# A 2-D transform and token update on one core: third stage on the four corners of the array, whole token rows stored, shorter loads, early scores for the last pair

## The chip, the core and the metric

The kernel runs on one of the cores of a Trainium2 chip. A core has five engines with queues of their own, executed in order: TensorE (PE, matrix multiplies into PSUM; its weight loads are shown as PEld), VectorE (DVE), ScalarE (ACT), GpSimd (POOL) and SyncE (SP, which here only issues DMAs). Sixteen DMA engines move data between HBM and SBUF. The metric is the device time of one execution in microseconds (us), the median of the runs.

## What is computed

```python
def _attn_ref(x):                      # x: (8, 3136, 256) float32
    X = np.fft.fft(x, axis=1)
    X = np.fft.fft(X, axis=2)
    return X.real.astype(np.float32)

def _moe_ref(x, w_gate, w1, w2, capacity):   # x is the transform, capacity 128
    scores = np.einsum('bsd,d->bs', x, w_gate)
    out = x.copy()
    for b in range(B):
        top_idx = np.argpartition(-scores[b], capacity)[:capacity]
        xe = x[b, top_idx]
        ye = np.maximum(xe @ w1, 0.0) @ w2
        g = 1.0 / (1.0 + np.exp(-scores[b, top_idx]))
        out[b, top_idx] = x[b, top_idx] + g[:, None] * ye
    return out
```

## The kernel before

The token axis of 3136 is split into 64 x 49, which needs no twiddle factors, so a batch passes three stages of matmuls, all in fp32. The input is laid out on the host: partitions are 98 rows (49 positions, twice) and 30 rows of zeros, and four tiles `x` of 1 MB make one batch.

- **Loads and folds.** `loads` brings the tiles over SP's queue into six buffers. `folds` adds the two mirrored halves of a tile (L319; DVE for batch 0, POOL for the others), in place.
- **Stage 1** (L346): per batch 66 pairs of matmuls, 128 rows x 64 columns, with `w1d` of 100 columns; the two of a pair write the upper and lower half of the PSUM partitions. ACT copies eight chunks to `uv` (L347, L349).
- **Stage 2** (L373): 25 values of k, two matmuls each (again the two halves of the columns) with `cuv` of 130 columns, three k in one PSUM bank. The copy to `s2` (L378) goes to DVE and ACT in turn.
- **Stage 3** (L389): one 128 x 128 matmul with 390 columns for each three k, with the table `mm`, which holds the 64 x 64 table `a` four times, `[[a, a], [-a, a]]`. ACT (L391) and DVE (L393) bring the two halves of the columns to the output buffer `o`; L393 adds the offsets `dl` that two small matmuls of stage 1 made.
- **Leave** (L412): twelve DMAs per batch write `o` to HBM, 64 partitions each and pieces of 512 bytes, half a token row. After them come the scores `sc` of the batch (L417), which one column of `o` holds, and their way to HBM and back (`spill`, `scr`, L419, L453), which spreads them for the search.
- **Search** (streams A to D, one for each pair of batches): six rounds of counting the scores over a threshold (ACT for A to C, L486; DVE for D, L489), a small matmul (L496) and a comparison; then the chosen rows' numbers are put in order (`chosen`, L584).
- **FFN** (streams a to d): the chosen rows are gathered from the output in HBM (L595), go through 96 matmuls of 256 columns and are scattered back (L642).

The order of all this is one string, `ORDER`: each letter lets one stream issue its next piece (l load, f fold, s, p, q stages 1 to 3, o leave, w weights, A to D, a to d). Every engine's queue follows from it. Stage 2 and stage 3 have two PSUM banks each.

Of the kernel before, what the change touches and what calls it, by code (L numbers as in the profile page):

```python
# [24 lines left out]
R = 132  # L25
LOW = 64 * K2
BIG = 3.0e38
RAD = {1: (16, 6), 2: (16, 6), 4: (8, 8)}
XBUFS, UVBUFS, OBUFS = 6, 2, 2
GROUPS = [[0, 1], [2, 3], [4, 5], [6, 7]]  # L30
PAIRS = [[0, 1], [2, 3], [4, 5], [6, 7]]
WARMS = 0
CORNERS = 4
TRIPLES = [(k, min(k + 3, K2)) for k in range(0, K2, 3)]
STORES = [(0, 9), (9, 18), (18, 25)]
ORDER = "3flflfl2slf2sl2slwfsl2fsfsl2psfq2s2p2fpfq2sp2qlpq2fqflso2sloqfsp2sqpfpfsqsqopsosl2f2pqpsofqs2posoqfposfsqlwl2qoqspf2psfofpqfpwsosql2qofpqp2olA2sfqsfqpAplqlspspqs2flAsoAslAlfqpfoAqwps2AospAfAf2qs2pAloslAwfqfqAoAfsos3Aopsqspf2qAf2pfpsAwqp2sqApAosfwpsoqwqpfsp2owqflaqowasqwof2spaqpqopsl2pfwsfqBlaqplflfqwaqpfpopBaqBqoqaplaBspsfalasofsBoaBaBsofsBlasBo2sq2oBapsBafBofpBsqfqpofqBsos2BafqoBpfs2aoBspaBqopCqBapBapCb2qoCsbf2qbopsbfsobqso2posbqCpCopCqCqoCpb2CpqaCqCbpoCqopCqobo2CbpC2qobCobobC3bCDbCbDbDbDcbc2Dc2Dc2D2c2Dc2Dc2Dc2DcbD2c2Ddcd6cdcd2c18d"
# [5 lines left out]

CHUNKS = [(1 + 4 * i, min(5 + 4 * i, 32)) for i in range(8)]
# [26 lines left out]
def _rows():  # L70

    p, c = np.arange(128)[:, None], np.arange(K2)[None]
    place = np.where(p >= 64, LOW + (p - 64) * (K2 - 1) + c - 1, p * K2 + c)
    k = np.arange(S)
    k1, k2 = k % NT, k % NB2
    mir = k2 >= K2
    return place, np.where(mir, LOW + -k1 % NT * (K2 - 1) + NB2 - k2 - 1, k1 * K2 + k2)


def _tables():  # L80
# [5 lines left out]
    t["w1d"] = np.concatenate([np.concatenate([c, -s, s, c], 1), np.concatenate([c, -s, -s, -c], 1), np.zeros((30, 100))], 0)  # L86
    d = np.arange(128)[:, None]
    k3 = np.array([0] + EO)[None]
# [4 lines left out]
    cu[:, 0] = 0  # L93
# [63 lines left out]
def kernel(ctx: ExitStack, tc: tile.TileContext, x, w1, w2, wgr, tb, outs, groups, pairs):  # L157
# [5 lines left out]
    xp = ctx.enter_context(tc.tile_pool(name="xp", bufs=XBUFS))  # L163
# [6 lines left out]
    ps3 = ctx.enter_context(tc.tile_pool(name="ps3", bufs=2, space=bass.MemoryType.PSUM))  # L170
# [4 lines left out]
    def bank(name, pool):  # L175
        return pool.tile([128, 512], F32, tag="bank", name=name)
# [8 lines left out]

    def loads():
        for b in range(NB):
            for i in range(4):
                t = xp.tile([128, 2, 8 * 128], F32, tag="x", name=f"x_{b}_{i}")
                src = x[4 * b + i].rearrange("p (c w) -> p c w", c=2)  # L190
                for c0, c1 in ((0, 1), (1, 2)) if b == 0 else ((0, 2),):
                    nc.sync.dma_start(t[:, c0:c1], src[:, c0:c1])  # L192
                    tiles[b, i] = t
                    yield True


    wz = cp.tile([128, 512], F32, tag="wz", name="wz")
    nc.vector.memset(wz, 0.0)
    wb = cp.tile([128, 128], BF16, tag="wb", name="wb")
    nc.vector.memset(wb, 0.0)  # L200

    pz = [bank(f"pz{i}", ps1) for i in range(2)]
    for i in range(CORNERS):
        for r in range(2):
            for c in range(2):
                h, w = (slice(64 * r, 64 * r + 64), slice(64 * c, 64 * c + 64))
                nc.tensor.matmul(pz[r][w, 0:260], wz[h, 0:64], wz[h, 64:324], start=True, stop=True)

    w1d = const("w1d", [128, 100], tb["w1d"], nc.scalar)
# [3 lines left out]
    load = loads()  # L213
    next(load)
    next(load)
    next(load)
    cuv = const("cuv", [128, 260], tb["cuv"])
    next(load)
    wgb = const("wgb", [128, 256 + 258], wgr.broadcast_to([128, 256 + 258]))
    next(load)  # L220
    zcs = const("zcs", [33, 256], tb["zcs"])
    mm = const("mm", [128, 128], tb["m"])
# [11 lines left out]

    obuf = [cp.tile([128, K2, R], F32, tag=f"o{i}", name=f"o{i}") for i in range(OBUFS)]
    dlt = [cp.tile([128, K2], F32, tag=f"dl{i}", name=f"dl{i}") for i in range(OBUFS)]
# [4 lines left out]
    wodd = cp.tile([128, 1], F32, tag="wodd", name="wodd")  # L241
    late, hots, se = {}, [], {}
# [15 lines left out]
    def late_setup():
        late["sm"] = const("sm", [128, SMW], tb["sm"])
# [459 lines left out]
```

## Time and profile before

| | us |
|---|---|
| median of 3 runs (284.11 to 285.78) | 284.39 |
| profiled execution | 284.24 |
| its span, first to last instruction | 282.5 |
| PE busy (with PEld beside it) | 239.5 (187.2) |
| DVE, ACT, POOL busy | 129.1, 120.1, 103.4 |

Busy time of PE is the union of its instructions, which are pipelined: a busy PE need not be at its peak. The profiled execution is 1.7 us longer than its span and stands 0.15 us below the median, so the span's times can be used for the median as they are. PE's granted clock is 2.4 GHz where the profile shows 1.0 (9 in tenths, also for a full slice) and 1.2 GHz where it shows 0.5.

### The profile page before, as it was taken

How to read it: one execution, taken by the hardware profiler on the slowest of the kernel's cores; microseconds unless marked ns; L12 is line 12 of the kernel's file. 1: busy time of each engine (PE TensorE's matmuls, PEld its weight loads, DVE VectorE, ACT ScalarE, POOL GpSimd, SP SyncE). 2: the span in 40 equal slices, each digit the busy share in tenths (PEclk: the TensorE clock that was granted, in tenths of full speed). 3: DMA queues.
4: the chain of work that ended last, by engine and by line, in shares of the span. 5: the costliest groups of instructions: out<-in, count | busy, mean ns of one | idle time of the engine just before them, and what ended most of it. 6: DMA issues, size and time to landing. Idle time of an engine off the chain costs nothing.

```text
span 282.5 us, 6641 instructions
## 1 busy us (share of the span) xinstructions
PE 239.5 (85%) x2604; PEld 187.2 (66%) x2604; DVE 129.1 (46%) x429; ACT 120.1 (43%) x292; POOL 103.4 (37%) x132
## 2 busy tenths in 40 slices
PE   4299999999986988999999899999897835568993
PEld 2297668767655665875779777767566724458893
DVE  0531222334325445756753265673557448762340
ACT  2064455545545674557546765234773001100220
POOL 0057953416037770590447471361000611002202
PEclk9579999999996899999999999999999975755998
DMA  6999899789999999999999999987888830000101
GB/s 230 408 421 392 331 240 283 227 236 321 264 298 391 379 367 352 298 225 232 285 346 347 303 277 263 246 224 179 210 194 214 209 97 20 0 0 19 41 19 37
DMA packets 61931, 66.55 MB, mean 236 GB/s; under 512 B 3947, under 2 KB 55884, under 8 KB 58316
## 3 DMA queue, kind: packets, MB, share of 16 engines
q1 hardware_dynamic: 60988, 63.99, 73.5%
q0 software_dynamic: 768, 2.10, 2.4%
q8 instruction: 20, 0.33, 0.5%
q10 hardware_dynamic: 144, 0.05, 0.1%
q14 instruction: 11, 0.09, 0.1%
HBM read 39.28 MB, written 26.84 MB: 234 GB/s over the span
## 4 chain that ended last, share of the span: by engine, by line
PE 32%; issue 23%; DMA 23%; POOL 8%; DVE 6%; ACT 4%; SPq 2%; POOLq 1%; DVEq 0%; ACTq 0%
DMA x<-in_x 15%; PE p L389 8%; PE p L373 8%; PE p L346 6%; DMA out<-o 5%; POOL x L319 4%; PE ph L230 2%; POOL hot L556 2%; PE ph L232 2%; PE ph L231 2%; DVE junk L489 2%; POOL out L642 1%; DMA spill<-sc 1%; ACT junk L486 1%; SPq L192 1%
## 5 line engine op out<-in xcount | busy, mean ns | idle before, releaser
L319 POOL TENSOR_TENSOR x<-x 128x512 f32<-128x512 f32 (+1 forms) x56 | 68.6, 1244 | 58.4 <-DMA x<-in_x 57.5
L346 PE MATMUL p<-w1d,x 128*64 128x100 f32 x1056 | 58.2, 262 | 8.8 <-DVE x L319 7.6
L346 PEld LDWEIGHTS p<-w1d,x 128*64 128x64 f32 x1056 | 50.9, 144 | 19.7 <-issue 14.5
L389 PE MATMUL p<-s,mm 128*128 128x390 f32 x144 | 59.1, 509 | 0.5 <-DVE o L393 0.5
L373 PE MATMUL p<-cuv,uv 128*64 128x130 f32 x800 | 57.3, 282 | 1.4 <-ACT uv L349 0.7
L373 PEld LDWEIGHTS p<-cuv,uv 128*64 128x64 f32 x800 | 44.0, 138 | 15.8 <-issue 8.7
L347 ACT COPY uv<-p 128x400 f32<-128x400 f32 x64 | 36.7, 578 | 39.8 <-PE p L346 36.1
L393 DVE TENSOR_TENSOR o<-p,dl 128x192 f32<-128x192 f32 (+1 forms) x72 | 24.2, 343 | 52.9 <-ACT o L391 51.3
L391 ACT COPY o<-p 128x198 f32<-128x198 f32 (+1 forms) x72 | 23.1, 329 | 30.3 <-PE p L389 26.2
L389 PEld LDWEIGHTS p<-s,mm 128*128 128x128 f32 x144 | 23.0, 192 | 15.1 <-issue 5.2
L378 DVE COPY s<-p 128x390 f32<-128x390 f32 x32 | 18.0, 563 | 25.5 <-PE p L373 25.1
L230 PE MATMUL ph<-xh,w1h 128*128 128x256 f32 x64 | 22.9, 358 | 4.4 <-DVE hl L630 3.5
L378 ACT COPY s<-p 128x390 f32<-128x390 f32 (+1 forms) x40 | 17.7, 441 | 16.2 <-PE p L373 15.6
L556 POOL TENSOR_TENSOR hot<-oa,sm 128x400 bf16<-128x400 bf16 x6 | 7.6, 1288 | 42.2 <-DVE oa L548 42.2
L230 PE MATMUL py<-w2h,hh 128*128 128x256 f32 x64 | 20.5, 321 | 2.0 <-DVE hl L630 1.4
L629 ACT ACTIVATE hh<-ph 128x512 fp32r<-128x512 f32 x16 | 9.5, 595 | 25.8 <-PE ph L232 23.2
L230 PEld LDWEIGHTS ph<-xh,w1h 128*128 128x128 f32 x64 | 13.7, 215 | 9.6 <-DVE hl L630 5.0
L232 PE MATMUL ph<-xl,w1h 128*128 128x256 f32 x64 | 20.0, 312 | 0.0
L595 POOL DMA_INDIRECT xe<-out,chosen x8 | 8.4, 1052 | 31.4 <-DVE chosen L584 28.9
L231 PE MATMUL ph<-xh,w1l 128*128 128x256 f32 x64 | 19.9, 311 | 0.0
L486 ACT ACTIVATE junk<-scr,thr 128x800 bf16<-128x800 f32 x18 | 17.3, 960 | 5.6 <-DVE thr L501 3.3
L630 DVE SCALAR_TENSOR_TENSOR hl<-ph,hh 128x512 fp32r<-128x512 f32 x16 | 11.1, 691 | 17.9 <-ACT hh L629 17.8
(117 smaller groups left out, 288.5 us busy)
## 6 DMA issues: line engine op xcount, KB each, us to landing
x<-in_x SPq DMA_DIRECT2D x28, 1024.0 KB, 10.6
out<-o SPq DMA_DIRECT2D x48, 288.0 KB, 7.0
out<-o SPq DMA_DIRECT2D x32, 224.0 KB, 5.1
x<-in_x SPq DMA_DIRECT2D x8, 512.0 KB
out<-o SPq DMA_DIRECT2D x16, 256.0 KB, 6.2
scr<-spill SPq DMA_DIRECT2D x8, 200.0 KB, 3.5
w1s<-in_w SPq DMA_DIRECT2D x1, 1024.0 KB
w2s<-in_w SPq DMA_DIRECT2D x1, 1024.0 KB
```

The source lines that it names most:

```text
L230: nc.tensor.matmul(out, ah, bh, start=start, stop=False)
L231: nc.tensor.matmul(out, al, bh, start=False, stop=False)
L232: nc.tensor.matmul(out, ah, bl, start=False, stop=stop)
L319: eng.tensor_tensor(t[:, 0 : n * 128], t[:, 0 : n * 128], t[:, n * 128 : 2 * n * 128], op=ALU.add)
L346: nc.tensor.matmul(ps[c : c + 64, q], t[:, s * 128 + c : s * 128 + c + 64], w1d, start=True, stop=True)
L347: nc.scalar.copy(uvt[:, :, :, :, a0:a1], src[:, :, :, :, 0:n])
L373: nc.tensor.matmul(ps[64 * h : 64 * h + 64, 130 * (k - k0) : 130 * (k - k0) + 130], uv[:, h, k], cuv[:, 0:130] if h else cuv[:, 130:260], ...
L378: (nc.vector.tensor_copy if k0 % 2 else nc.scalar.copy)(s2[:, 0 : 130 * n], ps[:, 0 : 130 * n])
L389: nc.tensor.matmul(ps, mm, mids.pop((b, k0))[:, 0 : 130 * n], start=True, stop=True)
L391: nc.scalar.copy(o[:, k0:k1, 0:R:2], pv[:, :, 0:66])
L393: nc.vector.tensor_tensor(o[:, k0:k1, 3:130:2], pv[:, :, 66:130], dl[:, k0:k1].unsqueeze(2).to_broadcast([128, n, 64]), op=ALU.add)
L486: nc.scalar.activation(junk, scr, AF.Sign, bias=thr, scale=-1.0, accum_out=ct)
```

## The change

- **Stage 3 on corners.** A 64 x 64 matmul uses one corner of the array: the upper or the lower rows, the left or the right columns. The table is now `a` alone, twice. For six k (two banks of stage 2) four corner matmuls of 390 columns make two products in two PSUM banks, `pp` and `pq`; ACT copies `pq` to `vt`, and DVE forms `pp - vt` and `pp + vt` into `o`, two instructions of 390 columns each. The two banks are all that stage 3 has: they have one buffer each, where the kernel before turned over two.
- **Offsets earlier.** The offsets are added as stage 2 leaves PSUM (ACT copies 65 columns of each k, DVE adds the offsets to the other 65). For batches 6 and 7 ACT does both.
- **Whole rows.** Rows of `o` and of the output have 260 elements. A batch leaves in six DMAs: two that write 1664 rows in runs of 7,280 or 6,240 bytes for each of 128 partitions, and four that write the 1536 mirrored rows in pieces of 520 bytes.
- **Loads without zero rows.** From batch 2 on, a tile's 98 rows are loaded alone (four DMAs of 64, 32, 1 and 1 rows, to every second, every fourth, and two single partitions); the six buffers keep the zeros of the first two batches.
- **Early scores.** For batches 6 and 7 the scores come from `uv` directly: 50 matmuls of one column, four corner matmuls, two DVE instructions, behind stage 1. Their `spill` goes out before the batch's stores.
- **Search D** counts half of the scores on ACT and half on DVE.
- **Beside these:** the residues of the weights are formed on POOL instead of DVE; 66 dummy bf16 matmuls stand at the start where 16 fp32 corner matmuls on zeros stood (L207); the score columns are made after the first folds; `ORDER` is another string.

```diff
 def loads():
+                if b < WHOLE: ...                                  # as before
+                else:
+                    f = t.rearrange("p c w -> p (c w)")
+                    r = 128 * 4 * WHOLE + 98 * (4 * (b - WHOLE) + i)
+                    nc.sync.dma_start(f[0:128:2], x[r : r + 64])
+                    nc.sync.dma_start(f[1:128:4], x[r + 64 : r + 96])
+                    for q in range(2):
+                        p = ROWS[96 + q]
+                        nc.sync.dma_start(f[p : p + 1]..., x[r + 96 + q : r + 97 + q]...)
 def stage1():
+            if b in EARLY:
+                ps = bank(f"pe_{b}", ps1)[:, 0:K2]
+                for k in range(K2):
+                    for h in range(2):
+                        c = 129 if h else 259
+                        nc.tensor.matmul(ps[64 * h : 64 * h + 64, k : k + 1], uv[:, h, k], cuv[:, c : c + 1], start=True, stop=True)
+                nc.vector.scalar_tensor_tensor(se_, zzb[b % 2], wodd, ps, op0=ALU.mult, op1=ALU.add)
+                yield True
...
+                scored(b)
 def stage3():
-                nc.tensor.matmul(ps, mm, mids.pop((b, k0))[:, 0 : 130 * n], start=True, stop=True)
-                nc.scalar.copy(o[:, k0:k1, 0:R:2], pv[:, :, 0:66])
-                nc.vector.tensor_tensor(o[:, k0:k1, 3:130:2], pv[:, :, 66:130], dl..., op=ALU.add)
+                pp, pq = (bank(f"p3{t}_{b}_{j0}", ps3, t)[:, 0 : R * n] for t in "pq")
+                for c in range(w // 64):
+                    s2 = mids.pop((b, j0 + c * (KH - 1)))
+                    for r, t in enumerate((pp, pq)):
+                        h = slice(64 * r, 64 * r + 64)
+                        nc.tensor.matmul(t[64 * c : 64 * c + 64], mm[h, 0:64], s2[h, 0 : R * n], start=True, stop=True)
+                nc.scalar.copy(vt, pq[0:w])
+                for h, op in enumerate((ALU.subtract, ALU.add)):
+                    nc.vector.tensor_tensor(o[0:w, j0:j1, h]..., pv, vv, op=op)
 def leave():
-                        nc.sync.dma_start(rows[s][h, :, k0 - s : z - s], o[p : p + 64, k0:z, 3 - h : 131 - h])
+                nc.sync.dma_start(rows[:, a:z], o[:, a:z].rearrange("p k h c -> p k (h c)"))
+                for h in range(2):
+                    nc.sync.dma_start(mirrored[h, :, m - 1 : z - 1], o[:, m:z, 1 - h])
```

In PE's queue, where batch 1 is in stages 2 and 3 and batch 2 in stage 1 (`p1_`, `p2_` and `p3_` are the PSUM tiles of the stages, the first number behind them the batch), the kernel before has one wide matmul of stage 3 at a time:

```order
L346 MATMUL p1_2_1_541<-w1d_114,x_2_0_285 64x100 x8
L389 MATMUL p3_1_0_551<-s2_1_0_522,mm_132 128x390
L373 MATMUL p2_1_3_557<-cuv_123,uv_1_313 64x130 x6
L346 MATMUL p1_2_2_566<-w1d_114,x_2_1_407 64x100 x8
L346 MATMUL p1_2_3_578<-w1d_114,x_2_1_407 64x100 x8
L373 MATMUL p2_1_6_593<-cuv_123,uv_1_313 64x130 x6
L373 MATMUL p2_1_9_602<-cuv_123,uv_1_313 64x130 x6
L389 MATMUL p3_1_3_611<-s2_1_3_564,mm_132 128x390
```

Now four corner matmuls stand together, behind two pieces of stage 2 of which they take the results, and serve six k:

```order
L428 MATMUL p2_1_1_683<-cuv_126,uv_1_352 64x130 x6
L428 MATMUL p2_1_13_693<-cuv_126,uv_1_352 64x130 x6
L377 MATMUL p1_2_4_703<-w1d_116,x4_93 64x100 x8
L428 MATMUL p2_1_4_715<-cuv_126,uv_1_352 64x130 x6
L460 MATMUL p3p_1_1_730<-s2_1_1_690,mm_130 64x390
L460 MATMUL p3q_1_1_731<-s2_1_1_690,mm_130 64x390
L460 MATMUL p3p_1_1_730<-s2_1_13_700,mm_130 64x390
L460 MATMUL p3q_1_1_731<-s2_1_13_700,mm_130 64x390
L428 MATMUL p2_1_16_740<-cuv_126,uv_1_352 64x130 x6
```

In SP's queue at the end, before (`out_6`, `out_7`: the output of batches 6 and 7; `spill` and `scr`: the scores' way; `scr_3`: those of search D):

```order
L412 DMA out_6<-o0_134 64x9x128 x2
L412 DMA out_6<-o0_134 64x8x128 x2
L412 DMA out_6<-o0_134 64x9x128 x4
L412 DMA out_6<-o0_134 64x7x128 x4
L419 DMA spill_146<-sc3_141 128x25
L412 DMA out_7<-o1_135 64x9x128 x2
L412 DMA out_7<-o1_135 64x8x128 x2
L412 DMA out_7<-o1_135 64x9x128 x4
L412 DMA out_7<-o1_135 64x7x128 x4
L419 DMA spill_146<-sc3_141 128x25
L453 DMA scr_3_2737<-spill_146 64x1x800 x2
```

and now, from the last tile's load on:

```order
L205 DMA x1_90<-in_x 64x2048
L206 DMA x1_90<-in_x 32x2048
L209 DMA x1_90<-in_x 1x2048 x2
L477 DMA out_6<-o0_134 128x1820
L481 DMA out_6<-o0_134 128x6x130
L358 DMA spill_146<-sc3_141 128x25
L526 DMA scr_3_2950<-spill_146 64x1x800 x2
L481 DMA out_6<-o0_134 128x6x130
L477 DMA out_6<-o0_134 128x1560
L481 DMA out_6<-o0_134 128x6x130 x2
L477 DMA out_7<-o1_135 128x1820
```

The scores of search D leave ahead of all stores of batch 7 and of most of batch 6, where they stood behind them; the last load stands directly before the first store of batch 6, where before all loads were out two batches of stores earlier.

## Rows read from the trace of the kernel before

**Rows 1.** The head of the page: the span, the busy times of the engines, and PE's granted clock in tenths in 40 slices of 7.06 us.

```profile
span 282.5 us, 6641 instructions
...
PE 239.5 (85%) x2604; PEld 187.2 (66%) x2604; DVE 129.1 (46%) x429; ACT 120.1 (43%) x292; POOL 103.4 (37%) x132
...
PEclk9579999999996899999999999999999975755998
```

**Rows 2.** Table by stretches: the stretch, its length, busy us of PE, PEld, DVE, ACT and POOL (with instruction counts), and last the granted clock, the mean busy share of the DMA engines and what they moved in GB/s. In the first two stretches only loads move, in the third loads and stores, in the last two stores (and the short transfers of a search).

```profile
7.00:16.00 9.00, 3.52 (x42) 3.54 (x44) 5.52 (x15) 1.14 (x2) 1.72 (x3) 0.55 1.04 411
18.50:27.00 8.50, 7.84 (x136) 6.63 (x132) 0.93 (x2) 4.61 (x12) 7.78 (x8) 1.00 1.03 396
60.20:69.50 9.30, 9.23 (x114) 7.03 (x114) 3.64 (x11) 4.66 (x12) 3.79 (x4) 1.00 1.00 321
192.00:207.40 15.40, 13.08 (x127) 9.29 (x124) 6.49 (x27) 10.32 (x28) 0.00 (x0) 1.00 0.85 205
208.60:223.00 14.40, 12.16 (x106) 9.82 (x106) 9.11 (x36) 5.52 (x15) 2.80 (x3) 1.00 0.85 205
```

**Rows 3.** The chain of work that ended last, pieces of PE: start, length, engine, line. Each fp32 matmul is two instructions, so x16 is a chunk of stage 1 (four pairs), x12 three k of stage 2, x2 three k of stage 3. x32, x24 and x4 are two pieces of one kind in a row.

```profile
73.14 1.37 PE p L346 x32
74.52 0.85 PE p L389 x2
75.37 0.84 PE p L346 x16
77.06 0.82 PE p L373 x12
...
99.33 1.33 PE p L373 x24
...
185.83 1.31 PE p L389 x4
```

**Rows 4.** Timeline of PE, three neighbouring matmuls of an FFN at full clock: start, length (they overlap), engine, line.

```profile
219.01 0.28 PE L232 MATMUL py<-w2l,hh 128*128 128x256 f32 x1
219.13 0.28 PE L230 MATMUL py<-w2h,hh 128*128 128x256 f32 x1
219.25 0.28 PE L231 MATMUL py<-w2h,hl 128*128 128x256 f32 x1
```

**Rows 5.** Groups of instructions by line: line, engine, operation, result and operands, shapes, count; busy us, mean ns of one; idle time before them and who ended it.

```profile
L389 PE MATMUL p<-s,mm 128*128 128x390 f32 x144 | 59.1, 509 | 0.5 <-DVE o L393 0.5
...
L378 DVE COPY s<-p 128x390 f32<-128x390 f32 x32 | 18.0, 563 | 25.5 <-PE p L373 25.1
L391 ACT COPY o<-p 128x198 f32<-128x198 f32 (+1 forms) x72 | 23.1, 329 | 30.3 <-PE p L389 26.2
L393 DVE TENSOR_TENSOR o<-p,dl 128x192 f32<-128x192 f32 (+1 forms) x72 | 24.2, 343 | 52.9 <-ACT o L391 51.3
L319 POOL TENSOR_TENSOR x<-x 128x512 f32<-128x512 f32 (+1 forms) x56 | 68.6, 1244 | 58.4 <-DMA x<-in_x 57.5
```

**Rows 6.** Weight loads of 64 columns and the matmuls of L207, min/median/max ns, then the first and the last start in us: first the 16 corner matmuls on zeros at the start (32 instructions), then stage 1 from 13 to 17.5 us (granted clock 0.5) and from 19 to 22 us (granted clock 1.0).

```profile
L207 PEld LDWEIGHTS pz<-wz x32: 178/227/227, 1.5 to 4.1; 64*64 64x64 f32 x32
L207 PE MATMUL pz<-wz x32: 380/637/692, 1.5 to 4.5; 64*64 64x260 f32 x32
...
L346 PEld LDWEIGHTS p<-w1d,x x56: 230/230/231, 12.8 to 17.4; 128*64 128x64 f32 x56
...
L346 PEld LDWEIGHTS p<-w1d,x x48: 132/137/137, 18.9 to 21.1; 128*64 128x64 f32 x48
```

**Rows 7.** Timeline of ACT: the last copy of stage 1 for batches 0, 3, 4 and 7 (start, length).

```profile
21.83 0.34 ACT L349 COPY uv<-p 128x100 f32<-128x100 f32 x1
...
82.12 0.33 ACT L349 COPY uv<-p 128x100 f32<-128x100 f32 x1
109.89 0.33 ACT L349 COPY uv<-p 128x100 f32<-128x100 f32 x1
...
193.02 0.34 ACT L349 COPY uv<-p 128x100 f32<-128x100 f32 x1
```

**Rows 8.** Timeline of SP's queue (start, length of the issues): the last load, the stores of batches 6 and 7, and the scores of batch 7.

```profile
167.10 0.70 SPq L192 DMA_DIRECT2D x<-in_x  x1
...
191.95 15.49 SPq L412 DMA_DIRECT2D out<-o  x12
...
208.50 14.58 SPq L412 DMA_DIRECT2D out<-o  x12
223.18 1.11 SPq L419 DMA_DIRECT2D spill<-sc  x1
224.34 3.39 SPq L453 DMA_DIRECT2D scr<-spill  x2
```

**Rows 9.** The chain of work that ended last, its end: first rounds of search D, `chosen`, the last gather, the end of the program.

```profile
230.81 1.07 DVE junk L489 x2
...
232.90 1.06 DVE junk L489 x2
...
257.71 0.18 DVE chosen L584
...
259.94 0.96 POOL xe L595
...
278.34 1.21 POOLq L715
```

**Rows 10.** The stores' time from issue to landing, us.

```profile
DMA to landing us min/median/max: 4.4/5.7/11.8
```

More of the change, by code (lines that the diff above doesn't have):

```diff
@@ L72, in _rows @@
     p, c = np.arange(128)[:, None], np.arange(K2)[None]
-    place = np.where(p >= 64, LOW + (p - 64) * (K2 - 1) + c - 1, p * K2 + c)
+    place = np.where(c < KH, p * KH + c, LOW + p * (KH - 1) + c - KH)
     k = np.arange(S)
@@ L76, in _rows @@
     mir = k2 >= K2
-    return place, np.where(mir, LOW + -k1 % NT * (K2 - 1) + NB2 - k2 - 1, k1 * K2 + k2)
+    q, j = np.where(mir, -k1 % NT, k1), np.where(mir, NB2 - k2, k2)
+    low = j >= KH
+    q, j = q + 64 * low, j - (KH - 1) * low
+    return place, np.where(mir, LOW + q * (KH - 1) + j - 1, q * KH + j)
 def _tables():
@@ L98, in _tables @@
     a[:33] = np.cos(2 * np.pi * ((n * k) % 64) / 64)
-    zc = a[:33].copy()
-    zs = -np.sin(2 * np.pi * ((n * k) % 64) / 64)
     n = np.arange(1, 32)[:, None]
     a[33:] = np.sin(2 * np.pi * ((n * k) % 64) / 64)
-    t["m"] = np.block([[a, a], [-a, a]])
-    t["zcs"] = np.concatenate([zc, zc, zs, zs], 1)
+    t["m"] = np.concatenate([np.concatenate([a, a], 0), np.where(np.arange(128) < 33, 1, -1)[:, None]], 1)
     p = np.arange(128)
@@ L184 @@
     tiles = {}
+    xbuf = [cp.tile([128, 2, 8 * 128], F32, tag=f"x{i}", name=f"x{i}") for i in range(XBUFS)]
     def loads():
@@ L213 @@
     load = loads()
+    for _ in range(6):
+        next(load)
+    cuv = const("cuv", [128, 260], tb["cuv"])
+    wgb = const("wgb", [128, 256 + 258], wgr.broadcast_to([128, 256 + 258]))
+    mm = const("mm", [128, 65], tb["m"])
     next(load)
     next(load)
[L216 to L222, printed above, removed]
     def smc(n):
@@ L359, in stage1 @@
-            nc.scalar.copy(dlt[b % OBUFS], pz[:, 1, 0:25])
-            yield True
+            pz = bank(f"pz_{b}", ps1)
+            nc.tensor.matmul(pz[32:64, 0:25], zs[b][:, 0:32], w1d[:, 50:75], start=True, stop=True)
+            nc.tensor.matmul(pz[0:33, 0:25], zs[b], w1d[:, 75:100], start=True, stop=True)
+            nc.scalar.activation(zzb[b % 2][0:64], pz[0:64, 0:25], AF.Copy, scale=mm[0:64, 64:65])
+            if b not in EARLY:
+                zw = zws[b] = sp.tile([64, K2], F32, tag="zw", name=f"zw_{b}", bufs=2)
+                nc.scalar.activation(zw, zzb[b % 2][0:64], AF.Copy, scale=wless[0:64])
@@ L495, in topk @@
             pc = sb[:, 144:160]
-            nc.tensor.matmul(pc[:, 0:rad], late[f"same{n}"], cth, start=True, stop=True)
+            for i in range(part):
+                nc.tensor.matmul(pc[:, 0:rad], late[f"same{n}"], cth[:, i], start=(i == 0), stop=(i + 1 == part))
             nc.vector.scalar_tensor_tensor(
-                ji, pc[:, 0:rad], enough, st.to_broadcast([128, rad]), op0=cmp, op1=ALU.mult, accum_out=inc
+                ji, pc[:, 0:rad], enough, st.to_broadcast([128, rad]), op0=ALU.is_le, op1=ALU.mult, accum_out=inc
             )
@@ L591, in ffn @@
         nm = f"{bs[0]}_0"
-        xe = fp.tile([128, n, D], F32, tag="xe", name=f"xe_{nm}", bufs=2)
+        xe = fp.tile([128, n, 2 * R], F32, tag="xe", name=f"xe_{nm}", bufs=2)
         gs = fp.tile([128, n], F32, tag="gs", name=f"gs_{nm}", bufs=2)
+        xw = [xe[:, i, 1 : 2 * R - 1].rearrange("p (c d) -> p c d", c=2)[:, :, 0:128] for i in range(n)]
         for i, b in enumerate(bs):
@@ L651, in keep_warm @@
         for i in range(WARMS):
-            for _ in range(8):
-                nc.tensor.matmul(sb[:, 0:128], wb, wb, start=True, stop=True)
+            warm(4, 256)
             yield True
-    streams = {"l": load, "f": folds(), "s": stage1(), "p": stage2(), "q": stage3(), "o": leave(), "w": late_setup(), "h": keep_warm()}
+    streams = {"g": score_columns(), "l": load, "f": folds(), "s": stage1(), "p": stage2(), "q": stage3(), "o": leave(), "w": late_setup(), "h": keep_warm()}
     for g, bs in enumerate(groups):
@@ L696, in _order @@
     for b, p in enumerate(parts):
-        out[b, :, 0:128] = p[first][:, 127::-1]
-        out[b, :, 128:256] = p[first][:, 128:256]
+        out[b, :, 0:128] = p[first][:, 128:0:-1]
+        out[b, :, 128:256] = p[first][:, R : R + 128]
     return out
```

246 lines of the change are left out of this document (145 added, 101 removed).

## Prediction

> **What bounds the kernel now.** I read the head of the page first: PE is busy for 85% of the span, no other engine for half of it, and the granted clock is full except at the start, around slice 13 and in the last quarter [rows 1]. So the question is whether PE's busy time is work or waiting. The chain of waits prices its pieces [rows 3]: two chunks of stage 1 in a row take 1.37 us, 0.685 each, but one between other work 0.84; six k of stage 2 take 1.33, 0.665 for three, alone 0.82; two wide matmuls of stage 3 take 1.31, 0.655 each, alone 0.85. So each change from one kind of matmul to another costs 0.16 to 0.19 us; I take 0.165. An FFN matmul takes 0.12 [rows 4].
>
> With these prices I sum PE's queue up to the end of stage 1 of batch 7. 528 matmuls of stage 1 are 66 chunks, 45.2 us. 175 k of stage 2 are 38.8. 56 wide and six narrow matmuls of stage 3 count as 58, 38.0. 96 FFN matmuls are 11.3. About a hundred small ones of the searches and offsets are an estimate of 7, at half an FFN matmul each. 149 changes of kind are 24.6. Together 165 us. The trace has 180: stage 1 begins at 12.8 [rows 6] and ends at 193.0 [rows 7]. Of the 15 that are missing, some 2.7 are the half clock at the start [rows 2], the rest waits, most of them between batches 3 and 4, where one batch takes 27.8 us [rows 7]. Up to there the kernel is bound by PE's work.
>
> The DMA engines run close behind. Where only loads move they bring 396 to 411 GB/s, where only stores move 205 [rows 2]; SP's queue shows 14.6 to 15.5 us for a batch's stores [rows 8]. By these prices a load of 1.05 MB takes 2.55 us. 32 loads are 82 us, the 4.8 batches of stores that stand before the last load 70, weights, tables and search rows 9, the start 3: 164, and the last load went out at 167.1 [rows 8]. So two resources are nearly full, PE the fuller at the end.
>
> From 193 on it is a chain of latencies. The scores of batch 7 stand behind its stores and leave at 223.2 [rows 8], the first round of search D begins at 230.8, `chosen` is there at 257.9, and the end, the last FFN, comes 24.6 us later [rows 1, 9].
>
> **The change, part by part.** *Stage 3.* That four corners work side by side is seen at the start [rows 6]: 16 corner matmuls of 260 columns begin within 3.0 us and are through some 0.4 later. The weight loads there took 227 ns, as stage 1's did at clock 0.5 (230) and not as at 1.0 (137), so this was half clock. A pair of stage 1, two halves with 100 columns, takes 0.171 at full clock, so 260 columns take 0.89 at half: four rounds of four give 3.6 us, eight rounds of two 7.1. The trace has the former. So four corner matmuls cost what one wide one did, 0.655, and serve six k. Up to the end of stage 1: 26 blocks and seven narrow ones at 0.22 are 18.5 us where 38.0 were.
>
> *The rest of PE's queue to that point.* Stage 1 unchanged, 45.2; 169 k of stage 2, 37.5; FFN 11.3; small ones 6.6; the early columns of batch 6, 50 fp32 matmuls of one column, not in the trace: below by an FFN matmul's half, 2.5 us, above by stage 2's rate for a matmul of 130 columns, 0.11, so 5.5; I take 2.5, since what is streamed is one column. 150 changes, 24.8. Sum 146.4. The dummies at the start, 18 of 512 columns and 48 of 256 at an FFN matmul's rate, are 9.9 us and 1.5 more for a first part at half clock; from 1.2 on they end at 12.6. So stage 1 begins no earlier, but at full clock. Losses were 12.5 beside the half clock; with lighter loads I take 5 (0 to 12.5). Stage 1 of batch 7 then ends at 12.6 + 146.4 + 5 = **164**, 29 us earlier than now.
>
> *DMA.* 98 rows of 8 KB are 0.80 MB, 1.95 us. A batch's stores are 1.60 MB in pieces of 520 bytes, at 205 GB/s 7.8 us, and 1.73 MB in runs of some 7 KB, which no store of the trace has: 4.2 us at the loads' rate (411), 8.4 at the stores' (205). I take 4.2, since the length of the run is the loads', and keep both: 12 to 16.2 for a batch. All six first batches' stores now stand before the last load: 8 x 2.55 + 24 x 1.95 + 6 x 12 + 9 + 3 = 151, up to 176 at the other end. With landing (5.7 [rows 10]), two folds (1.24 each [rows 5]) and the last two chunks the end of stage 1 comes no earlier than 160 by the low price, 186 by the high one. By the low one PE still decides. The two single-row loads of each tile are 8 KB each: at most two issues more, covered while SP's queue waits for the DMA engines.
>
> The trace's stores start on the SBUF side at any multiple of 4 bytes and on the HBM side at multiples of 512; the new pieces start at odd places on both sides. The Trainium skill, page "DMA: Bandwidth & Descriptors", section "How a descriptor splits into AXI transactions", says that a piece that does not start on a 256-byte boundary pays for the bytes below its start as well. By an estimate from that, 20 beats against 16, the 520-byte pieces would take 9.8 us a batch for 7.8, the loads would be out at 163 and the time be some 8 us longer; no run here shows it.
>
> *DVE, ACT and POOL.* In stage 3 DVE has two instructions of 390 columns for six k, 0.56 each [rows 5], where it had two of 192 at 0.34; in stage 2 it adds 195 columns at 0.34 for every three k where it copied 390 for every other. Per batch that is 8 us for 5.2, so some 151 us in all, of 240. ACT gives up about what it gets. POOL takes eight residues at 1.24, 10 us, beside the folds. None of them becomes the bound on average; what they hold up is a rival below.
>
> *The tail.* From the end of stage 1 of batch 7 (T) PE has about 10 us of queue up to the early scores' last product: the 50 columns, FFN sets, two pieces of stage 2, small search matmuls. `spill` leaves at about T + 12 instead of 30 us after T. To the first round it is 7.6 us as before, T + 20; the place of the round's matmul in PE's queue gives T + 22, a start of the round at T + 20.7. From round 1 to `chosen` it took 27.1. Splitting the count halves 1.07 us [rows 9], but ACT's half still has its two short follow-ups, so at most 0.4 a round, 2.4; against it stand stages 2 and 3 of batch 7, some 6 us of PE between rounds 5 and 6, of which I charge 3.5. `chosen` at T + 49. The stores of batch 7 must have landed before the gather: last block of stage 3 at T + 41, 2 for ACT and DVE, three issues at 1.2 [rows 8], 5.7 to land, T + 52, where the gather would issue at T + 51: one more. The last FFN as now, 24.6: end at T + 74.6 = 238.6, and the execution lies 1.7 over its span. **240 us**. Its profiled execution stands 0.15 under the median, so the sum holds for the median. By the bounds: T from 159 to 168 with a tail of 68 to 78 gives 229 to 248.
>
> **Rivals.** *The DMA engines become the bound.* If long runs go to HBM no faster than short ones, T is 186 and the time 262; halfway it is 250. For it: DMA share 1.0 in mixed stretches [rows 2]; no long store is in the trace. Against: the same engines move 8 KB runs twice as fast the other way.
>
> *The corners work only two at a time* with PE's other work around them, so that the change does not do what it says: 18.5 us more to T and 4 behind it, 262. Against: rows 6.
>
> *Stage 3 waits for its two banks* (the slow side). A block's banks come free after ACT's copy (0.56), DVE's two (1.12) and the hand-overs, 2 us after the matmuls. By the prices above PE has 1.7 to 12 us of other work between two blocks, 3.1 in the middle; only two of the 39 gaps are under 2. If DVE and ACT, busier than now, deliver late, each gap that is shorter stalls PE: release after 3 us costs 10 us over the run, after 4.5 47, after 5 63. From 4.5 on the kernel is slower than before; at 5 it takes 303. For it: one buffer where there were two, and in-order queues with search and FFN pieces between. Against: stage 3's matmuls waited for L393 only 0.5 us in the whole run, though ACT and DVE served them one after the other [rows 5].
>
> *More than forecast:* no losses before T and a shorter tail, 224 to 229.
>
> **How the numbers follow.** The forecast case, PE's sum decides, 229 to 248: 0.62. DMA bound, 248 to 262: 0.14. Corners by two, 262: 0.06. Banks: 0.06 for 250 to 280, 0.04 for slower than now. Better than 229: 0.06. A gain eaten up to within 1%: 0.02. The range of 8 in 10 leaves out the far ends: 228 to 259. One per cent, 2.8 us, is about what a measurement of this kernel can tell from no change; faster by more 0.93, within it 0.02, slower 0.05.
>
> **What would show it.** In the new profile: blocks of four corner matmuls at 0.65 to 0.85 us; the last copy of stage 1 at 160 to 168; loads-only and stores-only stretches with the rate of the long runs; PE's waits for DVE ahead of stage 3 of a few us in sum; `spill` of batch 7 some 12 us behind stage 1, `chosen` near 213, and 25 us from there to the end. Wrong it would be by a store rate under 250 GB/s, by waits of stage 3 for its banks of more than 10 us, or by a PE queue that waits for a search whose rounds come late, since a round's matmul blocks all behind it; or by a half clock in the last FFN, which costs 11 us there (96 matmuls at 0.12 more).

## Result and the profile after

The changed kernel takes 262.26 us (median, 261.70 to 262.57) beside 284.74 for the kernel before on the same chip: a ratio of 0.9205 (95% interval 0.9171 to 0.9239). I had said 240, with a range of 228 to 259. The sign is right, the gain is half of what was forecast. Below, the time of an experiment is the median of all runs of a kernel, and a ratio takes only those within 1.5% of its fastest; e5 and e13 have one such run each (246.33 and 243.27) and so no ratio. The head of the page after, for [rows 1]: the span, the busy times, and the granted clock and the DMA engines' share in 40 slices of 6.5 us.

```profile
span 260.7 us, 7635 instructions
PE 229.1 (88%) x3012; PEld 180.9 (69%) x3012; DVE 140.3 (54%) x461; ACT 135.1 (52%) x360; POOL 111.6 (43%) x144
PEclk9999999999997999999599998589979999998899
DMA  6999799999989999999899999681501981982001
```

PE is 88% busy where it was 85%, and the DMA share is at nine tenths or more in nearly every slice up to 160 us. The forecast failed ahead of one point, the end of stage 1 of batch 7, as ACT's last copies of stage 1 tell (start, length; batches 5 to 7, for [rows 7]):

```profile
118.76 0.33 ACT L380 COPY uv<-p 128x100 f32<-128x100 f32 x1
...
153.04 0.34 ACT L380 COPY uv<-p 128x100 f32<-128x100 f32 x1
...
187.00 0.35 ACT L380 COPY uv<-p 128x100 f32<-128x100 f32 x1
```

Forecast was T = 164; it is 187.0, 23 us later. Behind it the tail is as forecast (SP's queue, then the chain):

```profile
199.20 0.33 SPq L358 DMA_DIRECT2D spill<-sc  x1
...
234.49 0.18 DVE chosen L660
```

`spill` goes out at T + 12.2 (said 12), `chosen` at 234.5 is T + 47.5 (said 49), and from there to the end it is 26.2 (said 25.6). So only the 23 us have to be explained. Two stretches hold them (columns as in [rows 2]):

```profile
14.00:110.00 96.00, 85.86 (x1408) 66.97 (x1406) 49.55 (x159) 57.62 (x143) 54.30 (x74) 0.98 1.02 314
110.00:180.00 70.00, 62.80 (x813) 48.93 (x809) 40.34 (x132) 40.05 (x104) 40.65 (x44) 0.88 0.94 263
```

PE stood idle for 10.1 and 7.2 us, 17.3 where I had charged 5; and the clock below full level took 0.02 x 96 + 0.12 x 70 = 10.3, charged with nothing. 12.3 and 10.3 are 22.6 of the 23. PE's work itself, 146.4, was summed right. Who let PE stand is told by its two longest sums of waits in the whole run (us, times, longest), the gathers of the FFN and the folds of late loads:

```profile
PE pxt L684 <- DMA xe<-out,chosen: 9.1, 4, 5.6
PE p L377 <- POOL x L342: 5.5, 4, 4.1
```

In the chain of work that ended last it is loads and stores to 118 us and then the longest of these gathers; its pieces there and right behind read

```profile
117.94 7.81 DMA xe<-out,chosen
125.75 0.04 issue
125.79 0.69 PE pxt L684 x2
126.48 1.50 PE p L428 x12
```

Three k of stage 2 take 1.50 here, at half clock, where [rows 3] has 0.82. And the early scores' single columns, 2.5 us in my sum, took 3.7, with three k of stage 2 at half clock right behind (timeline of PE):

```profile
158.57 3.75 PE L397 MATMUL pe<-cuv,uv 128*64 128x1 f32 x100
162.18 1.55 PE L428 MATMUL p<-cuv,uv 128*64 128x130 f32 x12
```

### The profile page after: what moved, and what is told of

It reads as the page before. It is cut to its first block, busy times and chain, and to the rows that moved or that the text cites. A ratio compares the mean times of both kernels' runs of the same rounds, so it can differ in the third digit from the quotient of the medians.

```text
span 260.7 us, 7635 instructions
## 1 busy us (share of the span) xinstructions
PE 229.1 (88%) x3012; PEld 180.9 (69%) x3012; DVE 140.3 (54%) x461; ACT 135.1 (52%) x360; POOL 111.6 (43%) x144
## 4 chain that ended last, share of the span: by engine, by line
DMA 50%; PE 29%; issue 9%; DVE 4%; SPq 3%; POOL 2%; ACT 1%; POOLq 1%; DVEq 0%; ACTq 0%
DMA x<-in_x 22%; DMA out<-o 16%; PE p L428 7%; DMA xe<-out,chosen 7%; PE p L377 5%; DMA w2s<-in_w 4%; PE p3p L460 4%; PE ph L243 3%; PE pe L397 3%; PE ph L245 2%; PE ph L244 2%; DMA out<-xe,chosen 2%; POOL out L723 1%; PE pxt L684 1%; POOL hot L632 1%
## 5 line engine op out<-in xcount | busy, mean ns | idle before, releaser
L465 DVE TENSOR_TENSOR o<-p3p,vt 128x390 f32<-128x390 f32 (+1 forms) x80 | 37.0, 504 | 30.2 <-ACT vt L462 28.7
L434 ACT COPY s<-p 128x195 f32<-128x195 f32 (+1 forms) x72 | 22.2, 311 | 23.9 <-PE p L428 22.1
L442 DVE TENSOR_TENSOR s<-p,zz 128x195 f32<-128x195 f32 (+1 forms) x54 | 18.2, 342 | 27.6 <-ACT s L434 27.1
L460 PE MATMUL p3p<-s,mm 64*64 64x390 f32 (+1 forms) x144 | 32.5, 501 | 0.3 <-DVE o L465 0.3
L460 PE MATMUL p3q<-s,mm 64*64 64x390 f32 (+1 forms) x144 | 32.5, 501 | 0.0
L560 ACT ACTIVATE junka<-scr,thr 128x800 bf16<-128x800 f32 (+1 forms) x24 | 21.1, 879 | 13.0 <-DMA scr<-spill 6.7
L462 ACT COPY vt<-p3q 128x390 f32<-128x390 f32 (+1 forms) x40 | 17.6, 440 | 14.1 <-PE p3q L460 13.1
L723 POOL DMA_INDIRECT out<-xe,chosen x8 | 8.0, 996 | 25.0 <-DVE xe L719 19.0
L244 PE MATMUL py<-w2h,hl 128*128 128x256 f32 x64 | 18.5, 290 | 0.0
L245 PE MATMUL py<-w2l,hh 128*128 128x256 f32 x64 | 18.5, 289 | 0.0
```

Of the source, the lines that this page charges most:

```text
L244: nc.tensor.matmul(out, al, bh, start=False, stop=False)
L245: nc.tensor.matmul(out, ah, bl, start=False, stop=stop)
L434: nc.scalar.copy(sv[:, :, 0:65], pv[:, :, 0:65])
L442: nc.vector.tensor_tensor(sv[:, :, 65:R], pv[:, :, 65:R], zzb[b % 2][:, k0 : k0 + n].unsqueeze(2).to_broadcast([128, n, 65]), op=ALU.add)
L460: nc.tensor.matmul(t[64 * c : 64 * c + 64], mm[h, 0:64], s2[h, 0 : R * n], start=True, stop=True)
L465: nc.vector.tensor_tensor(o[0:w, j0:j1, h].rearrange("p n (c e) -> p n e c", e=2), pv, vv, op=op)
```

## Experiments

Theory 1: the DMA engines set the pace up to 126 us. Theory 2: PE's queue does, with the half clock behind the columns and the waits in order. Ratios below are to the kernel before, run on the same chip; the changed kernel's is 0.9205.

**Loads left out** (e1). In `loads()`:

```
 else:
+    yield True
+    continue
```

> Leaves out the loads of batches 2 to 7 (the buffers keep what is in them), so that only the stores and small transfers move; all else stays. Theory 1, the DMA engines set the time of the first half: stage 1 of batch 5 ends near 100 us where it ended at 118.8, that of batch 7 at 165 to 172 where it ended at 187.0, the whole 240 to 247. Theory 2, PE's own sum with the half clock behind the early columns sets it and the DMA waits are incidental: stage 1 of batch 7 ends at 180 or later, the whole 255 to 262.

249.97 us, ratio 0.8791 (0.8685 to 0.8897). Batch 5 ends at 106.5 in place of 118.8, batch 7 at 173.8. So 13 of the 23 us go with the loads, and 10 do not (the stores still move in this run): a result between the theories, nearer to the first. The same two stretches, without loads:

```profile
14.00:110.00 96.00, 91.16 (x1514) 70.25 (x1508) 55.74 (x181) 63.63 (x160) 63.87 (x85) 1.00 0.81 240
110.00:180.00 70.00, 65.73 (x886) 53.48 (x886) 38.54 (x140) 42.26 (x113) 32.00 (x36) 0.87 0.38 108
```

Idle time fell from 17.3 to 9.1, of which 4.9 are one wait for a gather; the clock's loss hardly moved (9.1).

**Long mirrored runs** (e5): what in the DMA time is it?

```
-for h in range(2):
-    nc.sync.dma_start(mirrored[h, :, m - 1 : z - 1], o[:, m:z, 1 - h])
+nc.sync.dma_start(mirrored[:, m - 1 : z - 1], o[:, m:z].rearrange("p k h c -> p k (h c)"))
```

> The mirrored tokens' rows are stored like the others, in runs of 6.2 to 7.3 KB by one DMA instead of two with 520-byte pieces; the swap of the two halves is left out, so mirrored tokens have their halves exchanged in the output. The same bytes, 5,888 fewer packets... for each pair of batches. If the first half is bound by the time that the pieces take on the DMA engines (a batch's mirrored rows about 8 us in pieces, about 4 in runs): the end of stage 1 of batch 5 moves from 118.8 to 103 to 108, that of batch 7 from 187.0 to 173 to 178, the whole 248 to 254, nearly what leaving out the loads gave (250). If only bytes count: 260 to 263.

(The count in that text is wrong: it is some 2,850 packets fewer for a batch.) 250.72 us (246.33 to 252.15), nearly all that leaving out the loads gave, though every byte still moves. Batch 5 ends at 110.7, later than I had expected, batch 7 at 176.6. So how the rows are cut costs far more here than their bytes.

**All pieces** (e10), the whole rows undone:

```
-nc.sync.dma_start(rows[:, a:z], o[:, a:z].rearrange("p k h c -> p k (h c)"))
+for h in range(2):
+    nc.sync.dma_start(rows[:, a:z, R * h : R * h + R], o[:, a:z, h])
```

> Undoes the whole token rows: the direct rows are stored in 520-byte pieces by two DMAs as the mirrored ones are; the same bytes, 3,072 pieces more for a batch and 256 runs fewer. The experiment with long mirrored rows took the same kind of piece away and gave 11.6 us. If pieces are priced so and the DMA engines decide: 273 to 285, stage 1 of batch 5 ends at 130 or later. If whole rows are worth nothing: 261 to 264.

298.59 us, ratio 1.0528 (1.0452 to 1.0604): slower than before the change, and by more than I expected. Without whole rows the new layout loses. SP's DMA queue on the page, with its packets, MB and its packets' time as a share of 16 engines' span, first after, then with long mirrored runs, then with all pieces, and last the kernel before:

```profile
q1 hardware_dynamic: 36336, 58.95, 75.6%
```
```profile
q1 hardware_dynamic: 13552, 58.95, 63.9%
```
```profile
q1 hardware_dynamic: 61168, 58.96, 84.6%
```
```profile
q1 hardware_dynamic: 60988, 63.99, 73.5%
```

Times their spans (260.7, 249.8, 295.4, 282.5) these are 197, 160, 250 and 208 us of all engines. The last two have the same number of packets: 520 bytes at odd places cost more than 512 at whole multiples.

**Whole tiles** (e2) and **rows on the first 98 partitions** (e6): are four DMAs a tile too many? (In e6 rows 96 and 97 come by a second DMA.)

```
-WHOLE = 2
+WHOLE = 8
```
```
-ROWS = list(range(0, 128, 2)) + list(range(1, 128, 4)) + [3, 67]
+ROWS = list(range(98))
...
+nc.sync.dma_start(f[0:96], x[r : r + 96])
```

> All tiles loaded as 128 rows in one DMA again, zero rows included: 0.25 MB more for each of 24 tiles, 0.6 us each at the loads' rate, but one DMA for each tile instead of four. If the bytes on the DMA engines set the first half: 18 tiles stand before 126 us, 8 to 12 us slower, 270 to 274. If the number of DMAs does (no more than eight of SP's are under way at a time, two tiles' worth): the same or faster, 252 to 262. If PE sets it: 262.

> The 98 rows of a tile lie on the first 98 partitions and come by two DMAs (96 rows of 8 KB, two rows in 1 KB pieces) instead of four; the same bytes. If the limit of eight of SP's DMAs under way starves the engines: 4 to 10 us faster, 252 to 258. If bytes and packets alone count: 261 to 264. If the place of the rows on the partitions counts (only the lower ones are written): slower, 264 to 270.

268.08 us, ratio 0.9359 (0.924 to 0.9479), and 270.41, ratio 0.9455 (0.9345 to 0.9565). Fewer DMAs did not help in either: bytes cost (6 us, less than the 8 to 12 expected), and so does the place of the rows (8 us). In e6 the same bytes hold the queue longer, 78.9% of 269.7, 213 us for 197:

```profile
q1 hardware_dynamic: 35952, 58.95, 78.9%
```

Among the packets' records an 8 KB row takes 462 ns on the mean there, 379 where the rows are spread over all partitions. With one DMA a tile over all 128 partitions (e2) it takes 358, so the number of DMAs is not what makes e6's rows slow.

**Wide columns** (e3), with loads, and (e15) without:

```
-nc.tensor.matmul(ps[64 * h : 64 * h + 64, k : k + 1], uv[:, h, k], cuv[:, c : c + 1], start=True, stop=True)
+nc.tensor.matmul(pw[64 * h : 64 * h + 64, 20 * k : 20 * k + 20], uv[:, h, k], cuv[:, c - 19 : c + 1], start=True, stop=True)
```

> The early scores' 100 matmuls stream 20 columns each instead of one, of which the last is used; nothing else changes. If the single columns make the clock fall: PE's clock stays at full level after them, 5 us less at 158 to 168 and 3 less at 188 to 194, and the whole takes 253 to 257. If the clock falls for another reason (the wait at the product behind them): 261 to 263.

> Leaves out the loads of batches 2 to 7, early scores in 20 columns: what is left over PE's sum of 164 when both the DMA engines' load and the single columns are gone. If the half clock at 146 to 158 us of the run without loads (about 5 us) came from the columns: stage 1 of batch 7 ends at 168 to 170, the whole 243 to 246. If not: 173 and 249 to 250.

258.69 us, ratio 0.9101 (0.9014 to 0.9189), and 245.44, ratio 0.8667 (0.8578 to 0.8757), against 249.97 for e1. From the start of each block of columns on, table by stretches, after and with 20 columns:

```profile
158.00:168.00 10.00, 9.74 (x169) 7.97 (x165) 4.72 (x21) 3.61 (x17) 3.34 (x3) 0.64 0.89 200
188.50:194.50 6.00, 6.00 (x114) 5.81 (x110) 3.19 (x18) 1.79 (x5) 0.00 (x0) 0.75 0.14 39
```
```profile
160.00:170.00 10.00, 9.17 (x203) 7.65 (x203) 5.87 (x24) 5.08 (x21) 5.46 (x5) 1.00 0.59 140
186.50:192.50 6.00, 5.75 (x128) 5.34 (x128) 3.54 (x19) 2.41 (x6) 0.00 (x0) 1.00 0.21 61
```

PE is no busier with 20 columns streamed in place of one, but the clock stays full. What let it fall was the single columns. The eleven traces that have them hold 22 such blocks, and in 20 the granted clock falls to half during the block or within 2 us behind it; batch 6 of e18 has no fall, and in e7 it had fallen ahead of batch 7's. In the eight traces with 20 columns it falls at none of the 16 blocks. The loss is 5 us in the two stretches shown, 3.6 of them ahead of T. At the end 3.6 came out, just at the edge of the intervals, and 4.5 without loads; T itself moved by 1.6 only (185.4), since as much half clock stands ahead of it at other places (10.2 us lost in both traces). Without loads the end of stage 1 of batch 7 came to 171.2, not quite the 168 to 170 expected: the gather's wait at 104 to 118 us stays (4.9 us, and half clock behind it).

**No corners** (e4), and the same **without loads** (e11): stage 3 on zero-padded weights of 128 rows.

```
-nc.tensor.matmul(t[64 * c : 64 * c + 64], mm[h, 0:64], s2[h, 0 : R * n], start=True, stop=True)
+nc.tensor.matmul(t[64 * c : 64 * c + 64], mab[:, r], s2[:, 0 : R * n], start=True, stop=True)
```

> Stage 3 with weights of 128 rows, half of them zeros, so that two column halves run side by side and no longer four corners; the same results. PE's sum to the end of stage 1 of batch 7 grows by some 18 us, and by 3 to 4 behind it. If PE sets the time all the way: 283 to 285. If the DMA engines set the time up to 126 us, what falls before that is hidden: 10 to 12 us, 272 to 275.

> Leaves out the loads of batches 2 to 7, and stage 3 runs on zero-padded weights without the four corners: to be compared with the run without loads (250). If the corners' gain (18 to 22 by the sum, 5.5 measured with the loads) is hidden behind the DMA engines: 266 to 272. If the corners themselves give no more than was measured: 254 to 258.

267.77 us, ratio 0.9422 (0.9346 to 0.9499): the corners give 5.5 us of 18 to 22. Without loads 258.73, ratio 0.9122 (0.9026 to 0.9217), 8.8 over e1: far from the first answer and, within the noise, at the end of the second. The end of stage 1 of batch 7 tells more: without corners it comes 1.7 us later with the loads (188.7 for 187.0) and 6.0 later without (179.8 for 173.8). So the loads hide a part of the gain, at that point the larger part. The chains of e1 and e11 show what a block costs, four corners and then two times two halves:

```profile
62.67 0.47 PE p3p L462
63.14 0.01 PE p3q L462
63.15 0.01 PE p3p L462
63.15 0.01 PE p3q L462
63.16 0.31 PE p3p L462
63.47 0.01 PE p3q L462
63.47 0.01 PE p3p L462
63.48 0.01 PE p3q L462
```
```profile
63.44 0.70 PE p3p L465 x4
64.14 0.66 PE p3q L465 x4
```

0.82 and 1.36 us: 0.54 a block, 14 us for the 26 wide blocks up to the end of stage 1. Only 6.0 of them reach that end, for the clock takes most of the rest: up to there half clock costs 8.5 us in e1 and 1.7 in e11. The second stretch of e11 has 0.98 where e1 has 0.87, 7.7 us in 70:

```profile
110.00:180.00 70.00, 65.50 (x851) 51.84 (x847) 41.77 (x138) 45.59 (x121) 38.86 (x43) 0.98 0.44 127
```

That the lighter queue is what lets the clock fall fits this, but is not shown. e11 has the single columns too, with 3.4 us of half clock behind those of batch 6 where e1 has 10.2; that e1's come from the columns is shown by e15.

**Order: later transposes** (e7), alone and with wide columns (e8). The transposes of FFN pairs 0 to 2 stand five to eight pieces later; nothing else moves. The piece of `ORDER` at pair 0 (`a`):

```
-wpapwqpBfapwqpaBaflsB
+w2pwqpBfpwaqpBflsaB
```

> Only the order is changed: the transposes of FFN pairs 0 to 2, which wait for the gathers with all of PE's queue behind them, stand five to eight pieces later. PE waited 9.1 us there, longest 5.6 at 120 to 126 us, and ran at half clock for some 4 us behind. If that wait delays the rest: 6 to 10 us faster, 252 to 256. If the pieces put ahead wait for loads themselves: 260 to 263.

> The later transposes together with the early scores in 20 columns. If the two losses are separate (3.6 us measured for the columns, 6 to 10 expected for the transposes): 248 to 253. If they overlap, since the DMA engines give the pace up to 126 us: 256 to 259.

272.72 us, ratio 0.9595 (0.9504 to 0.9687), and 272.31, ratio 0.961 (0.9504 to 0.9715): both theories of these texts fall. Stage 1 ends at 117.8 for batch 5 and 187.7 for batch 7 (e8: 119.3 and 186.4), as without the edit. That does not show that the wait for the gather cost nothing, for another wait took its place. In the changed kernel PE stands up to 125.8 for the gather; in e8 it stands up to 126.6 for DVE (timelines of PE, DVE and POOL in e8, then of DVE in the changed kernel):

```profile
126.57 0.48 PE L461 MATMUL p3p<-s,mm 64*64 64x130 f32 x1 [3.82 <-DVE s L443]
...
121.63 4.54 DVE L357 TENSOR_TENSOR sc<-sc,sm 128x1 f32<-128x1 f32 x1
...
120.00 2.50 POOL L330 TENSOR_TENSOR w1l<-w1s,w1h 128x512 fp32r<-128x512 f32 x2
122.45 3.69 POOL L330 TENSOR_TENSOR w2l<-w2s,w2h 128x512 fp32r<-128x512 f32 x3
```
```profile
121.01 4.30 DVE L357 TENSOR_TENSOR sc<-sc,sm 128x1 f32<-128x1 f32 x1
```

Stage 3 waits for `s`, and DVE's step for `s` stands behind an addition of one column (L357), which takes 0.16 us at its shortest and 4.54 here, until POOL's last residue ends at 126.1. The changed kernel has the same long step, but there the gather hides it. The residues came to POOL with this change; leaving them on DVE was not tried.

The tail grew: `chosen` came at T + 59.8 (e8: T + 55.9) in place of T + 47.5. There the work of FFN pairs 1 and 2 now stands later among the rounds of the last search; which wait of it costs most was not taken apart. Half clock is a part of it, 10.2 us up to `chosen` in e7 and 5.1 in e8 where the changed kernel has 1.7. In e7 that stretch has its clock at 0.83, where the changed kernel's tail had 0.96:

```profile
187.70:247.50 59.80, 50.14 (x494) 41.09 (x493) 36.12 (x136) 26.29 (x87) 7.34 (x7) 0.83 0.40 114
```

**One engine for the last search** (e12, `part = 1`) and **no dummies** (e18, `HEAD, WARMS = 0, 0`).

> The last search counts on ACT alone, as the others do. By the prediction's step the split is worth at most 0.4 us a round, 2.4 in all: chosen 1 to 3 us later, 262 to 265. If the split only adds hand-overs: 260 to 262.

> Leaves out the dummy matmuls at the start (18 of 512 columns, 48 of 256). The prediction took them to save 2.7 us of half clock in stage 1 of batch 0 and to begin it no earlier. If the DMA engines give the pace of the first half, the 2.7 us are hidden: 261 to 263, stage 1 of batch 5 ends at 118 to 120. If they are not hidden: 264 to 266.

263.35 us, ratio 0.9263 (0.9173 to 0.9353), and 261.64, ratio 0.9204 (0.9139 to 0.9268). The first differs by less than its interval. The second is no change (batch 5 ends at 118.3), though stage 1 of batch 0 runs at a clock of 0.70 from 13 to 20 us without dummies and at 1.00 with them: this loss of PE at the start is hidden, as theory 1 has it.

**A better version** (e13, e9, e14, e16, e17). e13 joins long mirrored runs, halves still exchanged, with wide columns. The others keep the results: the FFN gathers and scatters each row as two half rows.

```
+view = outs[b].rearrange("r (h c) -> (r h) c", h=2)
+return [(t[:, R * h : R * h + R], view, halves[h][:, b : b + 1]) for h in range(2)]
```

e9 works the half-row index out in four DVE steps, e14 takes it from the search's tables; both in batches 0 to 5. e16 does so in batches 0 to 3, e17 in 0 and 1.

> Long mirrored runs (the swap of the halves left out, so mirrored tokens are exchanged in the output) together with the early scores in 20 columns, and nothing on GpSimd's queue or in the search is added. Alone they gave 11.6 and 3.6 us. If the losses are separate: 245 to 248, stage 1 of batch 7 ends at 172 to 175. If one covers the other: 250 to 252.

> Batches 0 to 5 store the mirrored rows in long runs with their halves exchanged, and the FFN's gathers and scatters fetch and put back each row as two half rows, with an index for each half (four short DVE steps for a pair's indices, one more indirect DMA for each gather and scatter); batches 6 and 7 as they are. The early scores in 20 columns. The same results. If the price of the 520-byte pieces (11.6 us measured) and of the single columns (3.6 us) add up and the added transfers are hidden: 246 to 250. If the added transfers on GpSimd's queue hold up the FFN pairs: 252 to 258.

> As the experiment with the swap at the gather, but the half-row index comes out of the search's tables (they hold twice the row and its mirror bit), so that two short DVE steps a pair do in place of four, with the swap in batches 0 to 5; the last pair has one short step more. The same results. If the DVE steps beside GpSimd's work held up that version (1.2 and 0.9 us for two of them where 0.1 to 0.2 is usual): 246 to 252. If the added gathers and scatters on GpSimd's queue did: 256 to 260 as before.

> As the version with the half-row index from the tables, but only batches 0 to 3 are stored with exchanged halves; pair 2, whose gathers and scatters lie in the tail, goes back to one of each for a row. The same results. If the doubled gathers and scatters behind the end of stage 1 of batch 7 cost the 4 to 5 us that stand there (chosen 52 us behind it where 47 is usual): 251 to 254. If the ones of pairs 0 and 1, ahead of the residues on GpSimd's queue, cost more: 256 to 259.

> The same with batches 0 and 1 only: two batches' pieces are gone (4 to 5 us of DMA time each), pair 0 alone has doubled gathers and scatters. If the pieces of the earliest batches count most: 252 to 256. If each batch counts alike: 255 to 258.

e13: 248.83 us (243.27 to 249.08), 1.9 under e5 where 3.6 would be the full sum; the runs of each spread by 6 us, so whether the two losses overlap stays open. e9: 259.57, ratio 0.9135 (0.9061 to 0.9208), above both answers. e14: 257.14, 0.9064 (0.901 to 0.9119). e16: **256.72, 0.9008 (0.8952 to 0.9064)**, faster than both kernels. e17: 258.23, 0.9106 (0.9039 to 0.9174). The wide columns are in all of these, and alone (e3) they have 0.9101 (0.9014 to 0.9189), which overlaps with each: what the long runs add to them is not clear of the noise. In e9 two of the four DVE steps stand in the chain with 1.20 and 0.94 us, between POOL's work:

```profile
105.99 1.20 DVE half L671
107.19 0.02 issue
107.21 0.94 DVE rc L672
```

In e14 two steps are left, one of which still takes 1.20 us, beside a fold on POOL; the whole is 2.4 us less, within the intervals. POOL's doubled transfers remain: 12 gathers and 12 scatters of 1 us, and a second scatter that waits for the first one's landing, as they write to the same tensor (line, shapes, count; busy us, mean ns; idle before them and who ended it):

```profile
L742 POOL DMA_INDIRECT out<-xe,half x12 | 11.9, 992 | 18.1 <-DMA out<-xe,half 13.5 <-DVE xe L737 3.5 <-issue 0.8
L691 POOL DMA_INDIRECT xe<-out,half x12 | 11.8, 980 | 12.1 <-DVE ji L581 6.8 <-DVE half L671 2.5 <-issue 2.5
```

Taking pair 2's out of the tail brought `chosen` from T + 51.8 back to T + 49.1 (e16). In e17 batch 5 ends at 110.9, as early as in e13, and batch 7 at 182.7 where e13 has 175.2; two waits of PE for gathered halves (5.6 us) and a clock of 0.85 in the second stretch lie between. How much of it is the transfers and how much the clock stays open.

## Why the prediction was wrong

*PE's sum* held: 146.4 us, with idle time and clock added, gives the measured end.

*The DMA sum* failed, at "98 rows of 8 KB are 0.80 MB, 1.95 us" and, with it, at "By the low one PE still decides". I summed 151 to the last load; it was issued at 171:

```profile
171.15 0.48 SPq L205 DMA_DIRECT2D x<-in_x  x1
171.67 0.59 SPq L206 DMA_DIRECT2D x<-in_x  x1
```

Up to that load the packets' records fill 171.0 us of all 16 engines, so they were hardly ever free. By the records (mean of the run) a row of 8 KB took 379 ns, so a tile of 98 rows 2.32 us where I took 1.95, and a whole one 3.03 for 2.55; runs of 7.3 and 6.2 KB 292 and 286 ns, 4.6 a batch where "I take 4.2" stands; pieces of 520 bytes 41.6 ns, 8.0 for 7.8; and weights, tables, search and FFN rows took 19 us where 12 stood with the start. The sum with these is 8 x 3.03 + 24 x 2.32 + 6 x 12.6 + 19 = 175. So the largest error is the loads, 13 us; then the rest, 7, and the stores, 4. The loads were priced where only loads move (411), and ran in stretches where stores move too: from 14 to 30 us, ahead of the first store, a row took 319 ns. For the kernel before the same wrong price had been made good by another: its pieces took 30.5 ns, 12.0 us a batch, where I charged 14.6 from SP's queue. That my sum met [rows 8] was no proof of its terms. The rival "DMA engines become the bound", 262, names the time measured, but its condition was not met: a long run moves 25 bytes a ns on an engine, a piece 12.5. That its number came out is chance. The corners by two name 262 as well and are refuted by e1's block above.

*The odd places.* Pieces took 41.6 ns after and 46.3 with all pieces, for 30.5 before. The Trainium skill, page "DMA: Bandwidth & Descriptors", section "How a descriptor splits into AXI transactions", has a piece pay for the bytes below its start: by the estimate of 20 beats against 16, 30.5 would become 38. The runs agree in direction and go beyond it on the mean; the medians, 31 and 32 for 27, stay below it, and contention is in the means too.

*Losses, "I take 5"*, failed: 17.3 of idle time, and 10.3 of half clock beside it, which the sum had at nothing. With the loads left out 9.1 of the idle time stay (e1), so about half of it goes with the loads; the largest wait of the rest is 4.9 for a gather. The bounds, 0 to 12.5, were taken from the kernel before.

*The early columns, 2.5 us*, were 3.7, and the clock behind them, which my sum left out, cost about 5 more in two stretches, 3.6 of them ahead of T.

*Corners* do run four at a time, 0.82 a block with its change of kind as I had priced it. What was wrong is their worth: a block of two halves costs 1.36 in e11, not the 1.475 of two wide matmuls and a change, and most of the freed time went into waits and half clock.

*The residues on POOL* were charged with 10 us of POOL and nothing elsewhere; a step of DVE beside them took 4.30 us (at e8's rows).

*Stage 3's banks*, the slow rival: refuted, PE waited 0.3 us for L465 in the whole run:

```profile
L460 PE MATMUL p3p<-s,mm 64*64 64x390 f32 (+1 forms) x144 | 32.5, 501 | 0.3 <-DVE o L465 0.3
```

*The tail* was right in both parts. *The split count*, at most 2.4: 1.1 us measured, within the noise. *The dummies* give the full clock as I said, and it is worth nothing here.

## What to carry to other kernels

Price a transfer in the traffic that it will run in, and add up the packets' own durations, not the rate of a stretch where its kind moves alone; a sum that meets the end of the old kernel can hide two wrong terms. When the busiest engine is made lighter by a tenth, look for what stands second with less than that to spare: here the DMA engines, and the clock, which was lower with the lighter queue. Ask of work that moves to another engine whom it holds up there, not only whether that engine has time. Make a change of layout and the change that pays for it together: the new layout in pieces alone would have been slower than the old one.

## What the runs showed of the hardware

A hundred matmuls of one column left PE at half clock though it never stopped, at 20 of 22 blocks; with 20 columns the block took about as long, and the clock fell at none of 16. The same rows of 8 KB cost 462 ns instead of 379 when they were put on 98 neighbouring partitions. Short DVE steps of 0.16 us took 1.20 and 0.94 in e9's chain, 4.30 in the changed kernel and 4.54 in e8, each beside a fold or residues on GpSimd and up to the end of one (126.17 and 126.14 in e8); no run took GpSimd's work away to try it.
